# The last stage of a three-stage kernel: tanh left out of the gate, one subtraction on another engine, the last product turned around

## The chip, the cores and the metric

One Trainium2 chip, one of its cores. The core has TensorE (PE, whose weight loads are listed apart as PEld), VectorE (DVE), ScalarE (ACT), GpSimd (POOL) and SyncE (SP), which here only issues transfers. The metric is the device time of one execution in microseconds (us); less is better.

## What is computed

```python
# attention: q, k, v, f_logit are 4 x 8 x 768 x 48
f = sigmoid(f_logit)
state[t] = f[t][:, None] * state[t-1] + outer(k[t], v[t]);  y[t] = q[t] @ state[t]
x = y.transpose(0, 2, 1, 3).reshape(3072, 384)
# first feed-forward, 384 -> 1536 -> 384
x2 = ((x @ w_a) * (x @ w_b)) @ w_out
# second feed-forward, 384 -> 2048 -> 384
h = x2 @ w_in
out = (h - tanh(h)) @ w_out2
```

The inputs are q, k and v of size 0.1 (normal), f_logit 2 plus 0.5 times a normal, and weights scaled by the root of their length.

## The kernel before

All matrix products of the two feed-forward parts run in a form that splits each float32 operand into a high and a low part of the type float32r; a product is then three matmuls, high by high, high by low and low by high. `mm_split` (line 150) issues these three, so nearly every matmul of the trace carries line 150 and is told apart by its tiles. In the trace's names the operand that moves through the array stands first and the stationary one second: `o<-w_p,gh` moves the weights and holds the gate's high half.

The program runs attention and the first feed-forward together, block by block, and writes x2 in its two halves to DRAM (`xs`). The weights of the second feed-forward (`w_i`, `w_p`) are brought into the split form during the last of those blocks. Then comes the last stage, which the change is about. It is written in program order with no scheduler: each engine takes its instructions in the order of the loop.

The last stage has 96 steps: 6 blocks `o` of 512 tokens, times 16 slices `m` of 128 of the 2048 hidden columns. Step `i`, in order:

- PE makes `h`, 128 hidden columns by 512 tokens, in one PSUM bank: 9 matmuls (3 slices of the contraction, 3 of the split), in banks 0 to 3 by turns.
- `gelm_f32` (lines 84 to 96) makes h - tanh(h). ACT computes u = h squared (L86), tanh (L87) and two squares for the polynomial (L88, L89). POOL makes a mask of u over a threshold (L90). DVE makes xu (L91), h - tanh (L92), the two polynomial products v1 (L93) and v2 (L94), and puts h - tanh in place of the polynomial where the mask is set (L95).
- `gelm_lo` for step i - 1 makes the halves: ACT copies to `gh` (L560), POOL subtracts to `gl` (L561). There are 4 buffers of each.
- `o_group` for step i - 4 (`LAG`) adds the last product into 4 PSUM banks, one for each 128 of the 512 tokens: the gate's halves are stationary, the 384 columns of `w_p` move; 12 matmuls. At m = 15 ACT copies the 4 banks to `ob` (L582), and SP writes each to the output (L584).

One `ob` holds 64 tokens of each of two rows of the batch, so a write to the output has a shape of 2 by 64 by 384. The output has a row for each token.

A flag `okf` says whether the chunked form of attention was safe (the smallest product of decays). It is computed in the last block of the first feed-forward; each engine reads it (L711) and, where it is 0, a slow exact path runs instead.

Of the kernel before, what the change touches and what calls it, by code (L numbers as in the profile page):

```python
# [28 lines left out]
def tile_kernel(ctx: ExitStack, tc: tile.TileContext, q, k, v, f, w_a, w_b, w_out, w_in, w_out2, out):  # L29
    nc = tc.nc  # L30
    B, H, S, D = q.shape
    NT, DM = out.shape
# [51 lines left out]
    def gelm_f32(h, tmp):  # L84
# [10 lines left out]
        nc.vector.copy_predicated(v2, mk.bitcast(I32), t)  # L95
        return v2
# [55 lines left out]
    with tc.manual_schedule(), ExitStack() as p1:  # L152
# [237 lines left out]
        r2 = const.tile([1, 1], F32, name="r2")  # L390

        def flag():
            pr = att_bank("pr")
            nc.tensor.transpose(pr[0:1, 0:128], r1, ident)
            nc.vector.tensor_reduce(r2, pr[0:1, 0:128], mybir.AxisListType.X, ALU.min)
            nc.vector.tensor_scalar(okf, r2, P_MIN, None, ALU.is_ge)
# [134 lines left out]
        for jb in moe1(None):  # L531
# [16 lines left out]
            if jb == NBLK - 1 and slot == 2:  # L548
                flag()
# [6 lines left out]

        def gelm_lo(g):
# [13 lines left out]
        def o_group(i):  # L571
            o, m = divmod(i, MF2)
            if m == 0:
                po[o] = [bank(4 + g, f"o{g}")[:, :DM] for g in range(4)]
            g = G2.pop(i)
            for tg in range(4):
                cs = slice(128 * tg, 128 * tg + 128)
                mm_split(po[o][tg], [t[:, cs] for t in g], W["p", m], m == 0, m == MF2 - 1)
            if m == MF2 - 1:
                for tg in range(4):  # L580
                    ob = gp2.tile([128, DM], F32, tag="ob", name="ob", bufs=4)
                    nc.scalar.activation(ob, po[o][tg], ACTF.Copy)  # L582
                    c, hb = divmod(4 * o + tg, 2)
                    nc.sync.dma_start(  # L584
                        out=out.rearrange("(b s) d -> b s d", b=B)[2 * hb:2 * hb + 2, CH * c:CH * (c + 1), :],
                        in_=ob)

        for i in range(NO * MF2 + LAG):
            g = None
            if i < NO * MF2:  # L590
# [3 lines left out]
                ph = bank(i % 4, "h")  # L594
# [4 lines left out]
                g = gelm_f32(ph, lambda tag: gp2.tile([128, 512], F32, tag=tag, name=tag))  # L599
# [4 lines left out]
            gprev = g  # L604
            if i >= LAG:
                o_group(i - LAG)


    def general_path():
# [4 lines left out]
        yb = dpool.tile([B, S, H, D], F32, name="yb")  # L614
        flat = [x.rearrange("b h t d -> (b h) t d") for x in (q, k, v, f)]
        with ExitStack() as p3:
# [3 lines left out]
            with tc.For_i(0, S, TG) as t0:  # L620
# [22 lines left out]
                for eg in range(NE):  # L643
                    for b in range(B):
                        r0 = BH * eg + H * b
                        nc.sync.dma_start(
                            out=yb[b, ds(t0, TG), :, DE * eg:DE * (eg + 1)].rearrange("t h e -> h t e"),
                            in_=YG[r0:r0 + H])

        with ExitStack() as p4:  # L650
# [17 lines left out]
            with tc.For_i(0, NT // 128, 1) as it:  # L668
                x = sp.tile([128, H, D], F32, name="x")
                nc.sync.dma_start(  # L670
                    out=x,
                    in_=yb.rearrange("b t h d -> (b t) h d")[ds(it * 128, 128)],
                )
                xT = sp.tile([128, KT, 128], F32, name="xT")
                for kt in range(KT):
                    pt = pp.tile([128, 128], F32, tag="t", name="pt")
                    nc.tensor.transpose(
                        pt, x.rearrange("p h d -> p (h d)")[:, 128 * kt:128 * (kt + 1)], ident)
                    nc.vector.tensor_copy(xT[:, kt], pt)
                py = [pp.tile([128, 128], F32, name=f"py{d}") for d in range(KT)]  # L680
                for m in range(MF):
                    cs = slice(128 * m, 128 * (m + 1))
                    pa = pp.tile([128, 128], F32, tag="a", name="pa")
                    pb = pp.tile([128, 128], F32, tag="b", name="pb")
                    for p_, w_ in ((pa, FA), (pb, FB)):
                        for kt in range(KT):
                            nc.tensor.matmul(p_, w_[:, kt, cs], xT[:, kt], start=(kt == 0), stop=(kt == KT - 1))
                    asb = sp.tile([128, 128], F32, name="asb")
                    g = sp.tile([128, 128], F32, name="g")
                    nc.vector.tensor_copy(asb, pa)  # L690
                    nc.vector.tensor_tensor(g, asb, pb, ALU.mult)
                    for d in range(KT):
                        nc.tensor.matmul(py[d], FO[:, m, 128 * d:128 * (d + 1)], g,
                                         start=(m == 0), stop=(m == MF - 1))
                x2 = sp.tile([128, KT, 128], F32, name="x2")
                for d in range(KT):
                    nc.vector.tensor_copy(x2[:, d], py[d])
                po = pp.tile([128, DM], F32, tag="a", name="po")
                for m in range(MF2):
                    ph = pp.tile([128, 128], F32, tag="b", name="ph")  # L700
                    for kt in range(KT):
                        nc.tensor.matmul(ph, FI[:, kt, 128 * m:128 * (m + 1)], x2[:, kt],
# [40 lines left out]
```

## Time and profile before

| | |
|---|---|
| median of 3 runs | 1111.75 us (1111.71 to 1111.95) |
| the profiled execution: its own span | 1110.9 us |
| PE busy | 1018.1 us, 92% of the span |
| DVE busy | 826.0 us, 74% |
| ACT busy | 515.1 us, 46% |
| POOL busy | 506.8 us, 46% |
| mean granted TensorE clock | 0.962 of full speed |

The median of the runs is 0.85 us above the profiled span. Busy is the share in which an engine executes something; matmuls overlap in the pipeline, so a busy PE is not yet a PE at its peak. The stage at the end, from 653 us on, has its own limits, and the whole span's shares don't tell them.

### The profile page before, as it was taken

To read this page: it belongs to the slowest core of one execution; us is meant where nothing else is said; L and a number is where in the kernel's file an instruction comes from. 1 tells how busy PE (TensorE), PEld (TensorE's weight loads), DVE (VectorE), ACT (ScalarE), POOL (GpSimd) and SP (SyncE) were. 2 spreads that over 40 slices of the span, in tenths; PEclk is the share of its full clock that TensorE was granted. 3 is DMA by queue.
4 is the path that set the end of the run, shared out by engine and by line. 5 is a ranking of instruction groups with operands and counts; after the bars stand their busy time and mean duration, and the time that the engine had idled before them with its cause. 6 is when DMAs were issued, how large, how long until landed. Compare 5 with 4: busy or idle time off the path is not lost. (4 is left out here: it accounts for less than half of the span.)

```text
span 1110.9 us, 17772 instructions
## 1 busy us (share of the span) xinstructions
PE 1018.1 (92%) x6728; PEld 850.5 (77%) x6728; DVE 826.0 (74%) x1135; ACT 515.1 (46%) x979; POOL 506.8 (46%) x383
## 2 busy tenths in 40 slices
PE   7688889999999999999998879979989899899992
PEld 4567667888888888888776668869989799798891
DVE  8998887544444644444279989999999999999991
ACT  4433334333433333333333256666666666666661
POOL 3344543121212121212246557767767666677660
PEclk9789899999999999999999989989999999999997
DMA  6554455311412321140054440100100101000000
GB/s 129 145 142 120 129 144 138 62 30 23 114 30 43 92 45 30 36 102 1 15 190 141 149 146 1 58 10 21 57 29 1 59 28 58 22 8 1 29 1 31
DMA packets 134125, 72.41 MB, mean 65 GB/s; under 512 B 104912, under 2 KB 123344, under 8 KB 134032
## 3 DMA queue, kind: packets, MB, share of 16 engines
q1 hardware_dynamic: 132592, 69.23, 23.0%
q10 hardware_dynamic: 1440, 1.97, 1.0%
q8 instruction: 55, 0.90, 0.3%
q14 instruction: 38, 0.31, 0.1%
HBM read 55.05 MB, written 14.16 MB: 62 GB/s over the span
## 5 line engine op out<-in xcount | busy, mean ns | idle before, releaser
L491 POOL TENSOR_TENSOR gl<-gf,gh 128x512 fp32r<-128x512 f32 x72 | 93.1, 1293 | 365.2 <-ACT gh L490 365.2
L150 PE MATMUL o<-w_p,gh 128*128 128x384 f32 x768 | 203.2, 346 | 21.7 <-ACT ob L582 20.8
L150 PE MATMUL h<-x,w_i 128*128 128x512 f32 x864 | 214.4, 393 | 0.0
L90 POOL TENSOR_SCALAR mk<-u 128x512 f32<-128x512 f32 x96 | 179.3, 1868 | 22.9 <-ACT u L86 22.3
L150 PEld LDWEIGHTS h<-x,w_i 128*128 128x128 f32 x864 | 161.2, 188 | 29.4
L561 POOL TENSOR_TENSOR gl<-v,gh 128x512 fp32r<-128x512 f32 x96 | 124.6, 1298 | 112.4 <-ACT gh L560 112.2
L150 PE MATMUL b<-x,w_b 128*128 128x512 f32 x648 | 165.7, 400 | 10.2 <-DVE gf L489 9.7
L150 PE MATMUL a<-x,w_a 128*128 128x512 f32 x648 | 167.9, 403 | 5.8 <-DVE x L380 3.0
L150 PEld LDWEIGHTS o<-w_p,gh 128*128 128x128 f32 x768 | 145.2, 194 | 31.6 <-ACT ob L582 23.0
L150 PE MATMUL y<-gh,w_o 128*128 128x512 f32 x432 | 156.6, 417 | 4.5 <-ACT gh L490 4.5
L150 PEld LDWEIGHTS b<-x,w_b 128*128 128x128 f32 x648 | 121.4, 191 | 38.9 <-DVE gf L489 13.3
L150 PEld LDWEIGHTS a<-x,w_a 128*128 128x128 f32 x648 | 120.6, 191 | 33.2 <-DVE x L380 3.5
L93 DVE SCALAR_TENSOR_TENSOR v<-v,xu 128x512 f32<-128x512 f32 x96 | 144.4, 1505 | 0.0
L150 PE MATMUL o<-w_p,gl 128*128 128x384 f32 x384 | 133.6, 348 | 1.7 <-POOLq L712 0.7
L490 ACT ACTIVATE gh<-gf 128x512 fp32r<-128x512 f32 x72 | 45.5, 632 | 174.5 <-DVE gf L489 174.5
L560 ACT ACTIVATE gh<-v 128x512 fp32r<-128x512 f32 x96 | 60.7, 632 | 120.0 <-DVE v L95 119.4
L489 DVE TENSOR_TENSOR gf<-asb,b 128x512 f32<-128x512 f32 x72 | 49.3, 685 | 78.6 <-PE b L150 51.0
L150 PEld LDWEIGHTS y<-gh,w_o 128*128 128x128 f32 x432 | 85.1, 197 | 24.2 <-ACT gh L490 5.0
L94 DVE SCALAR_TENSOR_TENSOR v<-v,v 128x512 f32<-128x512 f32 x96 | 84.8, 883 | 10.0
L484 ACT ACTIVATE asb<-a 128x512 f32<-128x512 f32 x72 | 42.6, 592 | 104.7 <-PE a L150 82.1
L150 PE MATMUL y<-gl,w_o 128*128 128x512 f32 x216 | 88.3, 409 | 0.6 <-POOL gl L491 0.6
L95 DVE COPY_PREDICATED v<-mk,t 128x512 f32<-128x512 int32 x96 | 76.9, 801 | 9.9
(106 smaller groups left out, 1550.2 us busy)
## 6 DMA issues: line engine op xcount, KB each, us to landing
wst<-in_moe_w_out_dram SPq DMA_DIRECT2D x28, 384.0 KB
x<-xs SPq DMA_DIRECT2D x12, 768.0 KB
wst<-in_moe_w_in_dram SPq DMA_DIRECT2D x16, 384.0 KB
Tv<-in_v_dram SPq DMA_DIRECT2D x48, 96.0 KB
xs<-oh SPq DMA_DIRECT2D x18, 256.0 KB
xs<-ol SPq DMA_DIRECT2D x18, 256.0 KB
out_dram<-ob SPq DMA_DIRECT2D x24, 192.0 KB
Tf<-in_f_logit_dram SPq DMA_DIRECT2D x44, 96.0 KB
```

Source lines behind the costliest of these rows:

```text
L90: nc.gpsimd.tensor_scalar(mk, u, TANH_THR2, None, ALU.is_gt)
L93: nc.vector.scalar_tensor_tensor(v1, v1, Q_Y1, xu, ALU.add, ALU.mult)
L94: nc.vector.scalar_tensor_tensor(v2, v2, Q_Y2, v1, ALU.add, ALU.mult)
L95: nc.vector.copy_predicated(v2, mk.bitcast(I32), t)
L150: nc.tensor.matmul(dst, l_, r_, start=(first and i == 0), stop=(last and i == 2))
L484: nc.scalar.activation(asb, pb, ACTF.Copy)
L489: nc.vector.tensor_tensor(gf, asb, pab[1], ALU.mult)
L490: nc.scalar.activation(gh, gf, ACTF.Copy)
L491: nc.gpsimd.tensor_tensor(gl, gf, gh.bitcast(F32), ALU.subtract)
L560: nc.scalar.activation(gh, g, ACTF.Copy)
L561: nc.gpsimd.tensor_tensor(gl, g, gh.bitcast(F32), ALU.subtract)
```

## The change

Four things are done to the last stage:

- the gate uses the polynomial alone (`gelm_small`): tanh, mask, subtraction and selection are left out. The square of h also gives its sum over the 512 tokens (`accum_out`), one column of `usum` for each step. Where the greatest of these sums is over the threshold, the flag is cleared and the slow exact path runs. The flag moves to the end of the stage (`flag_rows` after step 96, `flag` one later);
- the subtraction to `gl` is made by DVE, no longer by POOL;
- the last product has the weights stationary and the gate's halves moving: 3 banks of 128 output columns by 512 tokens, 9 matmuls of 512 columns. `h` gets 5 banks;
- the output is stored transposed, 384 rows of 3072 tokens in the order of the blocks; each write is 128 rows by 512 tokens. The order of the tokens is put back outside the device's time.

The slow path is adapted to the new layout; it is not shown.

```diff
+    def gelm_small(h, tmp, total):
+        u, v1, v2, xu = (tmp(x) for x in ("u", "v1", "v2", "xu"))
+        nc.scalar.activation(u, h, ACTF.Square, accum_out=total)
+        nc.scalar.activation(v1, u, ACTF.Square, bias=bias1)
+        nc.scalar.activation(v2, u, ACTF.Square, bias=bias2)
+        nc.vector.scalar_tensor_tensor(xu, u, Q4, h, ALU.mult, ALU.mult)
+        nc.vector.scalar_tensor_tensor(v1, v1, Q_Y1, xu, ALU.add, ALU.mult)
+        nc.vector.scalar_tensor_tensor(v2, v2, Q_Y2, v1, ALU.add, ALU.mult)
         return v2
...
-        def flag():
-            pr = att_bank("pr")
-            nc.tensor.transpose(pr[0:1, 0:128], r1, ident)
+        def flag_rows(usum):
+            nc.vector.tensor_reduce(ru, usum, mybir.AxisListType.X, ALU.max)
+            nc.vector.scalar_tensor_tensor(ru, ru, TANH_THR2, r1, ALU.is_le, ALU.mult)
+
+        def flag(pr):
+            nc.tensor.transpose(pr[0:1, 0:128], ru, ident)
             nc.vector.tensor_reduce(r2, pr[0:1, 0:128], mybir.AxisListType.X, ALU.min)
-            nc.vector.tensor_scalar(okf, r2, P_MIN, None, ALU.is_ge)
+            nc.vector.tensor_scalar(okf, r2, 0.5, None, ALU.is_ge)
...
-            if jb == NBLK - 1 and slot == 2:
-                flag()
+                nc.vector.tensor_scalar(r1, r1, P_MIN, None, ALU.is_ge)
...
             nc.scalar.activation(gh, g, ACTF.Copy)
-            nc.gpsimd.tensor_tensor(gl, g, gh.bitcast(F32), ALU.subtract)
+            nc.vector.tensor_tensor(gl, g, gh.bitcast(F32), ALU.subtract)
             return gh, gl
 
         LAG = 4
+        NHB = 5
...
             if m == 0:
-                po[o] = [bank(4 + g, f"o{g}")[:, :DM] for g in range(4)]
+                po[o] = [bank(NHB + d, f"o{d}") for d in range(KT)]
             g = G2.pop(i)
-            for tg in range(4):
-                cs = slice(128 * tg, 128 * tg + 128)
-                mm_split(po[o][tg], [t[:, cs] for t in g], W["p", m], m == 0, m == MF2 - 1)
-            if m == MF2 - 1:
-                for tg in range(4):
-                    ob = gp2.tile([128, DM], F32, tag="ob", name="ob", bufs=4)
-                    nc.scalar.activation(ob, po[o][tg], ACTF.Copy)
-                    c, hb = divmod(4 * o + tg, 2)
-                    nc.sync.dma_start(
-                        out=out.rearrange("(b s) d -> b s d", b=B)[2 * hb:2 * hb + 2, CH * c:CH * (c + 1), :],
-                        in_=ob)
+            for d in range(KT):
+                cs = slice(128 * d, 128 * d + 128)
+                mm_split(po[o][d], [t[:, cs] for t in W["p", m]], g, m == 0, m == MF2 - 1)
+                if m == MF2 - 1:
+                    ob = gp2.tile([128, 512], F32, tag="ob", name="ob", bufs=3)
+                    nc.scalar.activation(ob, po[o][d], ACTF.Copy)
+                    nc.sync.dma_start(out=out[128 * d:128 * (d + 1), 512 * o:512 * (o + 1)], in_=ob)
...
-                ph = bank(i % 4, "h")
+                ph = bank(i % NHB, "h")
...
-                g = gelm_f32(ph, lambda tag: gp2.tile([128, 512], F32, tag=tag, name=tag))
+                g = gelm_small(ph, lambda tag: gp2.tile([128, 512], F32, tag=tag, name=tag), usum[:, i:i + 1])
...
+            if i == NO * MF2 + 1:
+                flag_rows(usum)
+            elif i == NO * MF2 + 2:
+                flag(bank(0, "pr"))
             if i >= LAG:
                 o_group(i - LAG)
...
-_OUTS = [((3072, 384), 'float32')]
+_OUTS = [((384, 3072), 'float32')]
```

The next rows are what the built programs hold, without any time. On VectorE, in the middle of the last stage, one step before:

```order
L91 SCALAR_TENSOR_TENSOR xu<-u,h 128x512
L92 TENSOR_TENSOR t<-h,t 128x512
L93 SCALAR_TENSOR_TENSOR v_7572<-v_7572,xu 128x512
L94 SCALAR_TENSOR_TENSOR v_7573<-v_7573,v_7572 128x512
L95 COPY_PREDICATED v_7573<-mk,t 128x512
```

and a step of the changed program, with the subtraction ahead of it:

```order
L576 TENSOR_TENSOR gl<-v_8296,gh 128x512
L103 SCALAR_TENSOR_TENSOR xu<-u,h 128x512
L104 SCALAR_TENSOR_TENSOR v_8361<-v_8361,xu 128x512
L105 SCALAR_TENSOR_TENSOR v_8362<-v_8362,v_8361 128x512
L576 TENSOR_TENSOR gl<-v_8329,gh 128x512
```

Five instructions have become four, and the fourth works on the gate of the step before.

On TensorE, the first step with a last product, before (the last `h` ahead of it, the product, and the next `h`):

```order
L150 MATMUL h<-x_5607,w_i_5814 128x512 x9
L150 MATMUL o_6476<-w_p_5665,gh 128x384 x2
L150 MATMUL o_6476<-w_p_5665,gl 128x384
L150 MATMUL o_6477<-w_p_5665,gh 128x384 x2
L150 MATMUL o_6477<-w_p_5665,gl 128x384
L150 MATMUL o_6478<-w_p_5665,gh 128x384 x2
L150 MATMUL o_6478<-w_p_5665,gl 128x384
L150 MATMUL o_6479<-w_p_5665,gh 128x384 x2
L150 MATMUL o_6479<-w_p_5665,gl 128x384
L150 MATMUL h<-x_5607,w_i_5857 128x512 x9
```

and now:

```order
L160 MATMUL h<-x_5605,w_i_5812 128x512 x9
L160 MATMUL o_6445<-gh,w_p_5663 128x512
L160 MATMUL o_6445<-gl,w_p_5663 128x512
L160 MATMUL o_6445<-gh,w_p_5663 128x512
L160 MATMUL o_6446<-gh,w_p_5663 128x512
L160 MATMUL o_6446<-gl,w_p_5663 128x512
L160 MATMUL o_6446<-gh,w_p_5663 128x512
L160 MATMUL o_6447<-gh,w_p_5663 128x512
L160 MATMUL o_6447<-gl,w_p_5663 128x512
L160 MATMUL o_6447<-gh,w_p_5663 128x512
L160 MATMUL h<-x_5605,w_i_5855 128x512 x9
```

Twelve matmuls of 384 columns have become nine of 512, and the gate is what moves.

On SyncE, the end of the program before (`x` loads of the last block, the last writes, the branch on the flag):

```order
L584 DMA out_dram<-ob 2x64x384 x4
L527 DMA x_9111<-xs_83 128x1536
L527 DMA x_9111<-xs_84 128x1536
L584 DMA out_dram<-ob 2x64x384 x12
L712 COMPARE_AND_BRANCH
```

and now:

```order
L541 DMA x_8515<-xs_83 128x1536
L541 DMA x_8515<-xs_84 128x1536
L598 DMA out_dram<-ob 128x512 x6
L736 TENSOR_LOAD okf
L736 ISA x2
L598 DMA out_dram<-ob 128x512 x3
L737 COMPARE_AND_BRANCH
```

The read of the flag now stands ahead of the last three writes; before, it stood much earlier.

## Rows read from the trace of the kernel before

**Rows 1.** The page: span, then busy us (share) xinstructions.

```profile
span 1110.9 us, 17772 instructions
PE 1018.1 (92%) x6728; PEld 850.5 (77%) x6728; DVE 826.0 (74%) x1135; ACT 515.1 (46%) x979; POOL 506.8 (46%) x383
```

**Rows 2.** Busy time, granted clock and DMA by window, within the last stage.

```profile
core 0: us, PE busy (x) PEld busy (x) DVE busy (x) ACT busy (x) POOL busy (x), PEclk, DMA share, GB/s
...
750.00:800.00 50.00, 50.00 (x252) 45.34 (x252) 47.72 (x57) 32.69 (x58) 35.84 (x23) 1.00 0.12 43
```

**Rows 3.** Who waited for whom, 660 to 1088 us: total, times, longest.

```profile
ACT gh L560 <- DVE v L95: 119.4, 85, 3.6
...
PE o L150 <- ACT ob L582: 20.8, 5, 8.2
```

**Rows 4.** Timeline of one step: start, duration, engine, instruction.

```profile
781.74 0.67 DVE L91 SCALAR_TENSOR_TENSOR xu<-u,h 128x512 f32<-128x512 f32 x1
...
782.33 0.68 DVE L92 TENSOR_TENSOR t<-h,t 128x512 f32<-128x512 f32 x1
...
782.59 1.29 POOL L561 TENSOR_TENSOR gl<-v,gh 128x512 fp32r<-128x512 f32 x1 [1.27 <-ACT gh L560]
...
782.93 1.51 DVE L93 SCALAR_TENSOR_TENSOR v<-v,xu 128x512 f32<-128x512 f32 x1
...
784.54 0.91 DVE L94 SCALAR_TENSOR_TENSOR v<-v,v 128x512 f32<-128x512 f32 x1
785.55 0.76 DVE L95 COPY_PREDICATED v<-mk,t 128x512 f32<-128x512 int32 x1
...
786.20 0.67 DVE L91 SCALAR_TENSOR_TENSOR xu<-u,h 128x512 f32<-128x512 f32 x1
```

**Rows 5.** Timeline, first and last step: v1 and v2 with POOL idle.

```profile
658.32 0.68 DVE L93 SCALAR_TENSOR_TENSOR v<-v,xu 128x512 f32<-128x512 f32 x1
...
1085.34 0.69 DVE L94 SCALAR_TENSOR_TENSOR v<-v,v 128x512 f32<-128x512 f32 x1
```

**Rows 6.** ScalarE's groups by line and shape, 630 to 1111 us: busy us, mean ns.

```profile
L88 ACT ACTIVATE v<-u,bias 128x512 f32<-128x512 f32 x96 | 69.6, 725 | 0.0
L89 ACT ACTIVATE v<-u,bias 128x512 f32<-128x512 f32 x96 | 69.4, 723 | 0.0
L560 ACT ACTIVATE gh<-v 128x512 fp32r<-128x512 f32 x96 | 60.7, 632 | 120.0 <-DVE v L95 119.4
...
L86 ACT ACTIVATE u<-h 128x512 f32<-128x512 f32 x96 | 56.5, 589 | 31.3 <-PE h L150 31.2
```

**Rows 7.** TensorE's timeline, a step of the last stage.

```profile
674.43 2.24 PE L150 MATMUL h<-x,w_i 128*128 128x512 f32 x9
676.51 0.52 PE L150 MATMUL o<-w_p,gh 128*128 128x384 f32 x2
...
678.61 2.24 PE L150 MATMUL h<-x,w_i 128*128 128x512 f32 x9
```

**Rows 8.** TensorE's timeline, first feed-forward: nine matmuls each of a, b, y.

```profile
560.49 2.22 PE L150 MATMUL a<-x,w_a 128*128 128x512 f32 x9
562.54 2.20 PE L150 MATMUL b<-x,w_b 128*128 128x512 f32 x9
564.58 0.39 PE L150 MATMUL y<-gh,w_o 128*128 128x512 f32 x1
...
566.62 0.62 PE L150 MATMUL a<-x,w_a 128*128 128x512 f32 x2
```

**Rows 9.** Timeline where the last stage starts: first x2 store, first h, first product.

```profile
651.78 0.33 SPq L465 DMA_DIRECT2D xs<-oh  x1
...
653.48 10.64 PE L150 MATMUL h<-x,w_i 128*128 128x512 f32 x45
...
663.96 0.51 PE L150 MATMUL o<-w_p,gh 128*128 128x384 f32 x2
```

**Rows 10.** The chain that ended last: start, us, what.

```profile
1089.00 2.02 PE o L150 x10
1091.02 0.02 issue
1091.04 0.49 ACT ob L582
```

**Rows 11.** Windows: x2's stores, and the end (last columns: clock, DMA share, GB/s).

```profile
652.00:653.00 1.00, 1.00 (x3) 0.77 (x3) 0.48 (x1) 0.56 (x1) 0.09 (x1) 0.50 0.38 145
...
655.00:656.00 1.00, 1.00 (x6) 0.81 (x5) 0.34 (x1) 0.00 (x1) 0.00 (x0) 1.00 1.02 375
...
1102.00:1104.00 2.00, 0.00 (x0) 0.00 (x0) 0.00 (x0) 0.00 (x0) 0.00 (x0) 0.50 0.13 51
...
1108.00:1109.00 1.00, 0.00 (x0) 0.00 (x0) 0.00 (x0) 0.00 (x0) 0.00 (x0) 0.50 0.05 17
```

More of the change, by code (lines that the diff above doesn't have):

```diff
@@ L31, in tile_kernel @@
     B, H, S, D = q.shape
-    NT, DM = out.shape
+    DM, NT = out.shape
     DFF = w_a.shape[1]
@@ L95, in gelm_f32 @@
         nc.vector.copy_predicated(v2, mk.bitcast(I32), t)
+        return v2
+    def gelm_small(h, tmp, total):
[6 more added lines that the diff above has]
+        nc.vector.scalar_tensor_tensor(v2, v2, Q_Y2, v1, ALU.add, ALU.mult)
         return v2
@@ L390, in tile_kernel @@
         r2 = const.tile([1, 1], F32, name="r2")
-        def flag():
-            pr = att_bank("pr")
-            nc.tensor.transpose(pr[0:1, 0:128], r1, ident)
+        ru = const.tile([128, 1], F32, name="ru")
+        def flag_rows(usum):
[3 more added lines that the diff above has]
+            nc.tensor.transpose(pr[0:1, 0:128], ru, ident)
             nc.vector.tensor_reduce(r2, pr[0:1, 0:128], mybir.AxisListType.X, ALU.min)
-            nc.vector.tensor_scalar(okf, r2, P_MIN, None, ALU.is_ge)
+            nc.vector.tensor_scalar(okf, r2, 0.5, None, ALU.is_ge)
         gens = {i: attn_step(i) for i in range(PRO + 1)}
@@ L555, in tile_kernel @@
         gp2 = p1.enter_context(tc.tile_pool(name="gp2", bufs=2))
+        usum = gp2.tile([128, (NT // 512) * MF2], F32, name="usum", bufs=1)
         def gelm_lo(g):
@@ L613, in general_path @@
         BH = B * H
-        yb = dpool.tile([B, S, H, D], F32, name="yb")
+        yb = dpool.tile([S // TG, B, TG, H, D], F32, name="yb")
         flat = [x.rearrange("b h t d -> (b h) t d") for x in (q, k, v, f)]
@@ L619, in general_path @@
             nc.vector.memset(S4, 0.0)
-            with tc.For_i(0, S, TG) as t0:
+            with tc.For_i(0, S // TG, 1) as ti:
+                t0 = ti * TG
                 LQ, LK, LF, LG = (fp.tile([128, TG, D], F32, name=nm) for nm in ("LQ", "LK", "LF", "LG"))
@@ L646, in general_path @@
                         nc.sync.dma_start(
-                            out=yb[b, ds(t0, TG), :, DE * eg:DE * (eg + 1)].rearrange("t h e -> h t e"),
+                            out=yb[ds(ti, 1), b, :, :, DE * eg:DE * (eg + 1)].rearrange("o t h e -> h (o t) e"),
                             in_=YG[r0:r0 + H])
@@ L667, in general_path @@
                         w_bits(dst[:, kk, c0:c0 + n0].bitcast(I32), st[:, :2 * n0])
[L668 to L685, printed above, removed]
-                        for kt in range(KT):
[L687 to L691, printed above, removed]
-                    for d in range(KT):
[L693 to L702, printed above, removed]
-                                         start=(kt == 0), stop=(kt == KT - 1))
-                    g = gelm_f32(ph, lambda tag: sp.tile([128, 128], F32, tag=tag, name=tag))
-                    nc.tensor.matmul(po, g, FP[:, m, :], start=(m == 0), stop=(m == MF2 - 1))
-                ob = sp.tile([128, DM], F32, name="ob")
-                nc.vector.tensor_copy(ob, po)
-                nc.sync.dma_start(out=out[ds(it * 128, 128), :], in_=ob)
@@ L740 @@
     r = _run(nc, [arrays], core_ids=[0])
-    got = tuple(r.results[0][f"out_{i}_dram"] for i in range(len(_OUTS)))
-    return got[0]
+    got = r.results[0]["out_0_dram"].reshape(384, 12, 4, 64)
+    return _np.ascontiguousarray(got.transpose(2, 1, 3, 0)).reshape(3072, 384)
```

47 lines of the change are left out of this document (added).

## The prediction

> **What bounds the kernel now.** I read the page first: PE is busy for 92% of the span [rows 1], which would make TensorE the bound. That is a mean over stages, so I went to the last stage alone. There DVE is busy 47.72 of 50 us while ACT has 32.69 and POOL 35.84 [rows 2]. PE counts as busy throughout, but its pipeline stretches the records of matmuls that wait; what decides is who waits for whom. ACT's copy to gh waits 119.4 us in all for DVE's last instruction of the gate [rows 3]. So the engine that never waits is DVE.
>
> The timeline of one step gives its pace: from one xu to the next, 781.74 to 786.20, are 4.46 us [rows 4]. 96 steps at 4.46 are 428 us. Of PE's own work a step holds nine matmuls of 512 columns, 674.43 to 676.51 or 2.08 us, and twelve of 384, to 678.61 or 2.10 us [rows 7]: 4.18 us. PE is thus only 0.28 us a step behind DVE, and that is the first thing to see: taking work from DVE can give no more than this before PE is the bound.
>
> The stage starts at 653.48 with 45 matmuls of h, the first product starts at 663.96 [rows 9], the last matmul ends at 1091.02 and the last copy at 1091.53 [rows 10]. Then 19.4 us pass to the end of the span in which no engine computes. The windows show why: the writes of the output move 51 GB/s with a DMA share of 0.13, about two of 16 engines, until after 1108 us, whereas the stores of x2, 128 rows by 512 columns, ran at 375 GB/s and a share of 1.02 [rows 11].
>
> **DVE's part.** Out go h - tanh, 0.60 us from start to start, and the selection, 0.65 us [rows 4]. In comes gl. What v1 costs is the point that needs care: it takes 1.51 us in a step, but it began while POOL's subtraction still ran, to 783.88, and ended 0.56 us after that [rows 4]; with POOL idle it took 0.68 us in the first step, and v2 took 0.69 us in the last [rows 5]. In the changed stage POOL has no work, so I take 0.69 us for each of the four: 4 x 0.69 = 2.8 us a step, against PE's 4.15. The bound from the other side is the stretched row: if v1 and gl, both with two operands in SBUF, cost 1.61 us from start to start and v2 1.01 whatever POOL does, a step has 0.59 + 1.61 + 1.01 + 1.61 = 4.82 us. The row with POOL idle is the nearer one.
>
> **ACT's part.** Tanh goes. Left are 0.59 + 0.73 + 0.72 + 0.63 = 2.67 us [rows 6], and 18 copies of a bank at some 0.6 us over the stage, 0.1 us a step. What the sum over the tokens adds to the square is in no row: between nothing and a further pass over the tile, 0.59 us. Even that leaves 3.4 us, under PE's step, so both ends cost nothing; from 1.4 us it would be the bound.
>
> **PE's part.** A step now has 18 matmuls of 512 columns. Nine take 2.08 us for h [rows 7]. For the new product, weights stationary and the gate moving, the nearest row is y of the first feed-forward, which has just this form: 564.58 to 566.62, 2.04 us; a and b there take 2.05 and 2.04 [rows 8]. Bounds are 2.04 and 2.10 us for nine; I take 2.075, nearer to the last stage's own row, as its engines are busier than the first's. Columns are the same in total as before (12 x 384 = 9 x 512), so the turned product itself gives nearly nothing; it pays through the stores. From the first product on there are 91 groups for h and 96 for o: 187 x 2.075 = 388.0 us (381.5 to 392.7). From 663.96 that ends at 1052.0, and 0.2 us for the flag's transpose and the last drain make 1052.2.
>
> The Trainium skill, page "TensorE: Matmul & The Clock Gate", section "Wait — 56ns, not 53.3ns?", gives 215.7 ns for a matmul of 512 columns at full clock, which as an estimate is 1.94 us for nine. The rows show 2.04 to 2.08 us, at a granted clock of 1.00 in the last stage [rows 2], which is the level of 2.4 GHz; they decide. By the page the stage would end 25 us earlier; that is a rival below.
>
> **What is hidden.** gl on DVE stands behind gh on ACT, which stands behind the next step's squares: square, two more squares, gh and gl are 0.59 + 0.73 + 0.72 + 0.63 + 0.69 = 3.4 us after the next h. The product that needs it comes three steps later, over 12 us, so neither is waited for. If ACT stalls, gh is late first, then gl, then the product. The flag's rows come after the last gl; their transpose stands ahead of the second-last product on PE. From the last h to that place PE has three products, 6.2 us; DVE needs some 4.5 us for the last gate and its gl and 0.5 for two small instructions. It is in time by about 1 us; if not, PE loses what is missing, below 1 us. Behind the flag's read on SP stand the last three writes; the flag is known a product earlier, 2 us ahead of the first of them, so the read is over. Without that cover the writes come later by about as much. The early flag's removal frees PE, DVE and SP of some 0.1 to 0.5 us; I count nothing.
>
> **The end.** The three copies of a block are now issued as each bank is done, so after the last matmul one copy of some 0.6 us is left. From the issue of x2's first store to data moving took about 0.85 us (651.78 to 652.6: the share in 652 to 653 is 0.38 [rows 9, 11]); 256 KB at 375 GB/s are 0.7 us. From the last data (about 1108.5 [rows 11]) to the end of the span were 2.4 us. 0.6 + 0.85 + 0.7 + 2.4 = 4.6 us against 19.9 now.
>
> **The sum.** 1052.2 + 4.6 = 1056.8, that is 54 us under the span of 1110.9: 39 from the step (96 x 0.3, the start and the stalls at the end of the stage) and 15 from the stores. The median of the runs lies 0.85 us over the span, which makes 1057.7, so 1058.
>
> **Rivals.**
> - Copies at the end of a block. The three banks of o are single, so the first product of a block waits for the copies of the last. Before, five such waits cost PE 20.8 us [rows 3], while DVE set the pace and they cost nothing; now each would count. Against it: the first copy is through about 3.3 us after h is ready (squares 2.0, gh 0.6, copy 0.6), and PE comes back to that bank after a product and the next h, 4.15 us. It decides when ACT is later than by 0.9 us. All of it: 1058 + 20.8 = 1079. The Trainium skill, "Perfetto Trace Analysis", section "Matmuls", says that independent groups of matmuls should rotate through banks so that emptying one overlaps the next group; these don't. By that rule the trace shows the waits, but not that they must stay. Chance 0.10.
> - The writes stay slow: rows of 512 tokens lie 12 KB apart in the output, and if they again use two engines, three writes of 256 KB at 51 GB/s take 15 us in place of about 1.5: 1072. Against it: x2's stores have such a stride too. Chance 0.06.
> - PE runs faster: if the extra 13 to 15 ns in each matmul come from traffic that the change takes away, nine take 1.94 us, and 187 x 0.135 = 25 us go: 1033. Against it: in the first feed-forward DVE was often idle, and nine still took 2.04. Chance 0.05.
> - DVE stays the bound and gets slower: the 4.82 us above. 96 x (4.82 - 4.46) = +35, less 15 for the stores: 1131. It decides where a step on DVE passes 4.46 + 15 / 96 = 4.62 us. Against it stand [rows 5]. Chance 0.03.
> - The flag falls and the slow path runs: it decides at a sum of squares over 0.4225 in any of the 96 columns. From the reference's inputs I work out at most 3.2e-5. The path has 768 steps of five DVE instructions at 0.68 us or more, over 2600 us more. Chance 0.01.
>
> **How the numbers follow.** The forecast has 0.75, with a range of its own of 1051 to 1064 (PE's bounds, 1 us for the flag, 2 for the end). Ends up to the slow writes and part of the copies' waits give 1048 to 1077, which leaves out PE's faster pace, most of the copies' case and the slow ones, together under 0.2. A measurement here tells 0.2%, 2.2 us, from no change. All cases but DVE and the flag are faster: 0.95; 0.01 for a pace that ends just where it was; 0.04 slower.
>
> **What would show it.** DVE under 70% busy in the stage, v1 near 0.69 us, POOL without work; groups of nine matmuls every 2.04 to 2.10 us without a gap from 664 us on; no wait of PE for ob; the writes of the output at a DMA share near 1; some 5 us from the last matmul to the end. A pace above 4.3 us a step, waits on L597 at block ends, or a tail of 15 us would make me wrong, each in its own term.

## The result and the profile after

The changed kernel takes 1060.79 us (median of four runs, 1058.78 to 1061.16); the kernel before took 1111.73 beside it. The ratio is 0.9535, with a 95% interval of 0.9519 to 0.9551. The forecast was 1058, with a range of 1048 to 1077. The profiled execution has a span of 1059.2 us in a run of 1060.94, so 1.7 us lie outside the span.

I read the last stage first, as before. The windows of the changed kernel (busy us of PE, PEld, DVE, ACT, POOL, then granted clock, DMA share and GB/s) show 50 us in the middle of the stage, and the end:

```profile
750.00:800.00 50.00, 50.00 (x220) 40.78 (x218) 32.40 (x49) 32.33 (x64) 0.00 (x0) 1.00 0.13 48
1052.00:1053.00 1.00, 1.00 (x5) 0.47 (x3) 0.00 (x0) 0.84 (x2) 0.00 (x0) 1.00 0.00 0
1053.00:1054.00 1.00, 0.00 (x0) 0.00 (x0) 0.00 (x0) 0.60 (x1) 0.00 (x0) 1.00 0.90 342
1054.00:1055.00 1.00, 0.00 (x0) 0.00 (x0) 0.00 (x0) 0.00 (x0) 0.00 (x0) 1.00 1.01 371
1055.00:1056.00 1.00, 0.00 (x0) 0.00 (x0) 0.00 (x0) 0.00 (x0) 0.00 (x0) 1.00 0.29 100
1056.00:1057.00 1.00, 0.00 (x0) 0.00 (x0) 0.00 (x0) 0.00 (x0) 0.00 (x0) 1.00 0.05 14
```

DVE fell from 47.72 [rows 2] to 32.40 of 50 us, and POOL has no instruction. In the tail the writes now move up to 371 GB/s at a share near 1, where it was 51 at 0.13 [rows 11]. Who waits for whom has turned round. The waits of 640 to 1060 us (total, times, longest):

```profile
ACT u L100 <- PE h L160: 133.3, 86, 1.6
DVE xu L103 <- ACT u L100: 113.2, 91, 1.4
ACT ob L597 <- PE o L160: 5.4, 1, 5.4
```

Before, ACT waited 119.4 us for DVE and PE 20.8 for ob [rows 3]. Now ACT waits for PE, DVE waits for ACT, and PE has no wait for ob at all. TensorE sets the pace. The groups of DVE and ACT in the stage (busy us, mean ns; then idle time before them):

```profile
L105 DVE SCALAR_TENSOR_TENSOR v<-v,v 128x512 f32<-128x512 f32 x96 | 66.5, 693 | 10.3 <-ACT gh L575 0.5
L104 DVE SCALAR_TENSOR_TENSOR v<-v,xu 128x512 f32<-128x512 f32 x96 | 66.5, 692 | 10.0
L103 DVE SCALAR_TENSOR_TENSOR xu<-u,h 128x512 f32<-128x512 f32 x96 | 66.0, 687 | 113.2 <-ACT u L100 113.2
L576 DVE TENSOR_TENSOR gl<-v,gh 128x512 fp32r<-128x512 f32 x96 | 65.9, 686 | 0.2 <-ACT gh L575 0.2
...
L101 ACT ACTIVATE v<-u,bias 128x512 f32<-128x512 f32 x96 | 69.6, 725 | 3.1
L102 ACT ACTIVATE v<-u,bias 128x512 f32<-128x512 f32 x96 | 68.1, 709 | 0.6 <-DVE gl L576 0.6
L575 ACT ACTIVATE gh<-v 128x512 fp32r<-128x512 f32 x96 | 59.2, 616 | 0.5 <-DVE v L105 0.5
L100 ACT ACTIVATE u<-h 128x512 f32<-128x512 f32 x96 | 57.5, 599 | 134.0 <-PE h L160 133.3
L100 ACT ACTIVATION_READ_ACCUMULATOR u<-h 128x1 f32 x96 | 18.6, 194 | 0.0
```

A step has 2.76 us on DVE (four instructions) and 2.84 on ACT. The last of the ACT rows answers the open price of the sum over the tokens: its read-out is an instruction of its own, 194 ns, and the square itself takes 599 ns where it took 589 [rows 6]. The timeline shows a step of PE (start, duration), and the flag at the end:

```profile
770.99 2.25 PE L160 MATMUL h<-x,w_i 128*128 128x512 f32 x9
773.07 0.39 PE L160 MATMUL o<-gh,w_p 128*128 128x512 f32 x1
...
775.16 2.22 PE L160 MATMUL h<-x,w_i 128*128 128x512 f32 x9
...
1047.13 0.16 DVE L405 SCALAR_TENSOR_TENSOR ru<-ru,r 128x1 f32<-128x1 f32 x1
...
1048.54 0.27 PE L408 MATMUL pr<-ident,ru 128*1 128x128 f32 x1
```

From h to h are 4.17 us here. The first product starts at 665.42 and the last matmul at 1052.60, which for 187 groups of nine is 2.070 us each. The flag's row is ready at 1047.29, 1.25 us before PE comes to the transpose. The chain that ended last (start, us, what) runs through PE without a gap to the last copy:

```profile
1042.45 6.26 PE o L160 x27
...
1048.82 4.20 PE o L160 x18
...
1053.03 0.60 ACT ob L597
```

From there to the end of the span are 5.6 us, where it was 19.4. The three writes of the last block, issued at 1052.26, 1052.96 and 1053.66, took ever longer to land (us; the first is the shortest, the last the longest):

```profile
DMA to landing us min/median/max: 2.0/2.8/3.6
```

### The profile page after: what moved, and what is told of

Its sections match the earlier page's. It is cut to its first block, busy times and chain, and to the rows that moved or that the text cites. A ratio compares the mean times of both kernels' runs of the same rounds, so it can differ in the third digit from the quotient of the medians.

```text
span 1059.2 us, 16687 instructions
## 1 busy us (share of the span) xinstructions
PE 997.1 (94%) x6438; PEld 801.2 (76%) x6440; DVE 674.5 (64%) x1042; ACT 485.2 (46%) x973; POOL 205.2 (19%) x191
## 4 chain that ended last, share of the span: by engine, by line
PE 79%; DVE 11%; issue 5%; DMA 2%; ACT 1%; POOL 1%; ACTq 0%; SPq 0%; DVEq 0%; POOLq 0%
PE o L160 19%; PE h L160 19%; PE y L160 11%; PE a L160 11%; PE b L160 10%; DVE wc L81 3%; DVE wc L80 3%; PE pt L281 2%; PE yy L376 2%; PE sc L332 1%; PE uu L359 1%; PE pk L336 1%; DVE wc L82 1%; DVE gf L503 1%; DVE PRE L308 1%
## 5 line engine op out<-in xcount | busy, mean ns | idle before, releaser
L160 PE MATMUL o<-gh,w_p 128*128 128x512 f32 x576 | 194.7, 393 | 0.0
L103 DVE SCALAR_TENSOR_TENSOR xu<-u,h 128x512 f32<-128x512 f32 x96 | 66.0, 687 | 113.2 <-ACT u L100 113.2
L160 PEld LDWEIGHTS o<-gh,w_p 128*128 128x128 f32 x576 | 108.2, 188 | 24.7 <-issue 0.2
L100 ACT ACTIVATE u<-h 128x512 f32<-128x512 f32 x96 | 57.5, 599 | 134.0 <-PE h L160 133.3
L160 PE MATMUL o<-gl,w_p 128*128 128x512 f32 x288 | 113.1, 393 | 0.0
L82 DVE SCALAR_TENSOR_TENSOR wc<-wst,wc 128x384 int32<-128x384 int32 x68 | 74.6, 1096 | 2.4
L105 DVE SCALAR_TENSOR_TENSOR v<-v,v 128x512 f32<-128x512 f32 x96 | 66.5, 693 | 10.3 <-ACT gh L575 0.5
L104 DVE SCALAR_TENSOR_TENSOR v<-v,xu 128x512 f32<-128x512 f32 x96 | 66.5, 692 | 10.0
L101 ACT ACTIVATE v<-u,bias 128x512 f32<-128x512 f32 x96 | 69.6, 725 | 3.1
```

The lines of the kernel that those rows point to most:

```text
L82: nc.vector.scalar_tensor_tensor(dst, lo, 29, dst, ALU.logical_shift_right, ALU.bitwise_or)
L100: nc.scalar.activation(u, h, ACTF.Square, accum_out=total)
L101: nc.scalar.activation(v1, u, ACTF.Square, bias=bias1)
L103: nc.vector.scalar_tensor_tensor(xu, u, Q4, h, ALU.mult, ALU.mult)
L104: nc.vector.scalar_tensor_tensor(v1, v1, Q_Y1, xu, ALU.add, ALU.mult)
L105: nc.vector.scalar_tensor_tensor(v2, v2, Q_Y2, v1, ALU.add, ALU.mult)
```

## The experiments

Times are medians, and the ratio is to the kernel before, on the same chip.

**One part alone.** Three runs take the change apart. `stores_only` leaves the kernel before as it is, but writes each bank in two halves of 64 rows.

```diff
-                    nc.sync.dma_start(
-                        out=out.rearrange("(b s) d -> b s d", b=B)[2 * hb:2 * hb + 2, CH * c:CH * (c + 1), :],
-                        in_=ob)
+                    for r in range(2):
+                        nc.sync.dma_start(
+                            out=out.rearrange("(b s) d -> b s d", b=B)[2 * hb + r, CH * c:CH * (c + 1), :],
+                            in_=ob[64 * r:64 * r + 64])
```

> The kernel before with one edit: each write of 2 by 64 by 384 is issued as two writes of 64 by 384, one for each row of the batch. Theory (a write whose outermost dimension is 2 keeps to two of the 16 DMA engines; that makes the tail): the DMA share at the end rises from 0.13 to well over 0.5, the time from the last matmul to the end falls from 19.9 to some 7 us, and the time to about 1098 (1095 to 1101). Rival (rows of 1536 bytes, or the place in the output, make the writes slow): the share stays near 0.13 and the time at 1111.

1103.55 us, 0.9926 [0.9904, 0.9948]. The transposed layout isn't needed for this part of the gain: a shape whose outermost size is 64 in place of 2 is enough to leave the slow writes. Its windows in the tail, and then the issues on SP:

```profile
1090.00:1092.00 2.00, 0.00 (x0) 0.00 (x0) 0.00 (x0) 0.24 (x1) 0.00 (x0) 1.00 0.51 120
1092.00:1094.00 2.00, 0.00 (x0) 0.00 (x0) 0.00 (x0) 0.00 (x0) 0.00 (x0) 0.75 0.68 160
```

```profile
1088.70 6.59 SPq L585 DMA_DIRECT2D out_dram<-ob  x8
```

The share is 0.51 to 0.68 instead of 0.13 [rows 11]. The time from the last matmul to the end is 12.0 us; 19.9 it was, and 7 were expected. SP issues the eight writes over 6.59 us, and the data end 1.3 us after the last issue; as far as the rows tell, the issuing is the limit now. The splitting didn't make it longer: the four writes of before were issued over 8.13 us. So the gain was nearly 9 us and not 14: right in kind, too large in size. The Trainium skill, "DMA: Bandwidth & Descriptors", section "Rules for kernel authors", says that an outermost dimension of c below 16 confines a transfer to at most c engines. The trace agrees: an outermost 2 gave a share of 0.13, about two of 16, and 128 gives 1.01.

`gate_only` is the kernel before with `gelm_small` and the late flag; the subtraction stays on POOL, product and stores stay as they were.

```diff
...
-                g = gelm_f32(ph, lambda tag: gp2.tile([128, 512], F32, tag=tag, name=tag))
+                g = gelm_small(ph, lambda tag: gp2.tile([128, 512], F32, tag=tag, name=tag), usum[:, i:i + 1])
...
+            if i == NO * MF2 + 1:
+                flag_rows(usum)
+            elif i == NO * MF2 + 2:
+                flag(bank(0, "pr"))
```

> The kernel before with only the gate by polynomial and the late flag; the subtraction stays on POOL, product and stores as before. Theory (DVE's five instructions set the pace, then PE does, and the tail is the stores'): a step falls from 4.46 to PE's 4.18 us, the last matmul ends near 1055, the tail stays at 19.9 us, the time is about 1076 (1072 to 1080). Rival one (the turned product earns PE time as well): a step stays above 4.25 us and the time above 1082. Rival two (POOL's subtraction goes on stretching v1 and so holds DVE): v1 stays at 1.5 us, which is 3.3 us a step for DVE in all, so that it would show in v1's mean and not in the time.

1076.70 us, 0.9678 [0.9661, 0.9694], as expected. This is the greater part of the change. The gate lost instructions on DVE, ACT and POOL at once, and they were not tried one by one; that DVE's are the ones that count is read from the trace of before, in which DVE goes from one step to the next without a wait [rows 4] and waits 1.8 us in all 96 gates together. The timeline of `gate_only`, DVE and POOL:

```profile
762.59 0.69 DVE L105 SCALAR_TENSOR_TENSOR v<-v,v 128x512 f32<-128x512 f32 x1
...
762.94 1.51 POOL L577 TENSOR_TENSOR gl<-v,gh 128x512 fp32r<-128x512 f32 x1 [2.68 <-ACT gh L576]
```

`product_only` is the changed kernel with the gate of before, its subtraction on POOL, and a flag that holds the decays alone.

```diff
...
-            nc.vector.tensor_tensor(gl, g, gh.bitcast(F32), ALU.subtract)
+            nc.gpsimd.tensor_tensor(gl, g, gh.bitcast(F32), ALU.subtract)
...
-                g = gelm_small(ph, lambda tag: gp2.tile([128, 512], F32, tag=tag, name=tag), usum[:, i:i + 1])
+                g = gelm_f32(ph, lambda tag: gp2.tile([128, 512], F32, tag=tag, name=tag))
```

> The changed kernel with the old gate (tanh, mask, selection) and the subtraction on POOL: only the turned product with its stores, 5 banks for h and the late place of the flag are left; the sum over the tokens is left out, and the flag tells of the decays alone. Theory: DVE's pace of 4.46 us a step as before, a tail of some 6 us: about 1098 (1095 to 1101). Rival (turning the product frees PE time that counts): under 1090.

1102.36 us, 0.9905 [0.9885, 0.9924], just above. DVE is back at 47.37 of 50 us and the step at 4.48. The 4 us missing are at the end, in PE's timeline and in the window of 1088 to 1092:

```profile
1088.28 0.37 PE L407 MATMUL pr<-ident,ru 128*1 128x128 f32 x1 [3.32 <-DVE ru L404]
1088.30 0.77 PE L160 MATMUL o<-gh,w_p 128*128 128x512 f32 x1
```

```profile
1088.00:1092.00 4.00, 3.73 (x10) 2.94 (x11) 0.64 (x4) 0.63 (x1) 1.27 (x1) 0.50 0.03 8
```

With DVE late, the flag's transpose waits 3.32 us, and both last products stand behind it on PE. The granted clock is then 0.50, the level of 1.2 GHz, so that the matmuls come every 0.43 us. SP's issue of the very last write took 1.80 us besides, where 0.33 is usual; why isn't known. The 1.25 us of margin of the changed kernel are what keeps the wait from it.

**The subtraction.** `gl_pool` is the changed kernel with this one instruction back on POOL (the first two changed lines of the diff above).

> The changed kernel with one edit: the subtraction to gl goes back to POOL. Theory (with the gate by polynomial DVE has over 1 us of slack a step, and gl is needed three steps later): no change, 1059 to 1063, though v1 grows from 0.69 us towards 1.5 where it meets POOL's subtraction. Rival (the moved subtraction is part of the gain, since POOL stretches DVE and gl comes late): PE waits for gl, and the time is above 1065.

1059.37 us, 0.9527 [0.9510, 0.9545]: the same as the changed kernel. But it didn't go as expected inside. Its groups in the stage:

```profile
L576 POOL TENSOR_TENSOR gl<-v,gh 128x512 fp32r<-128x512 f32 x96 | 143.0, 1490 | 251.4 <-ACT gh L575 251.4
...
L105 DVE SCALAR_TENSOR_TENSOR v<-v,v 128x512 f32<-128x512 f32 x96 | 66.4, 692 | 10.1 <-ACT v L102 0.2
```

v1 doesn't meet POOL's subtraction here at all; v2 does, ahead of it by 0.35 us as in `gate_only` (764.55 against 764.90), and v2 keeps its 692 ns. It is POOL's subtraction that grows, from 1.29 [rows 4] to 1.49 us. Before, gl began at 782.59 and v1 at 782.93, and v1 waited [rows 4]; in `gate_only` v2 began at 762.59 and gl at 762.94, and gl waited. The trace of before has both orders behind the end of a block:

```profile
751.17 0.69 DVE L93 SCALAR_TENSOR_TENSOR v<-v,xu 128x512 f32<-128x512 f32 x1
...
751.53 1.48 POOL L561 TENSOR_TENSOR gl<-v,gh 128x512 fp32r<-128x512 f32 x1
...
751.96 1.60 DVE L94 SCALAR_TENSOR_TENSOR v<-v,v 128x512 f32<-128x512 f32 x1
```

The subtraction, second to v1, takes 1.48 us, and v2, second to the subtraction, 1.60. Of these pairs the instruction that comes second pays. The Trainium skill says this of these two engines ("SBUF — State Buffer", section "Who interferes with whom"): a DVE instruction with two inputs in SBUF contends with a GpSimd instruction that reads SBUF, and the order of issue decides who blocks. The traces agree for v1, v2 and the subtraction. Before, v2 also ran beside POOL's mask, from 783.85 to 785.78: it took 0.91 us and ended ahead of it [rows 4], so that pair shows no waiting for the other's end.

**How much room ACT has.** In the changed kernel ACT has 2.84 of 4.14 us. `act_2` adds two passes of 0.53 us to each step, between the squares and gh; `act_4` adds four. The output doesn't use them.

```diff
         nc.scalar.activation(v2, u, ACTF.Square, bias=bias2)
+        for k in range(2):
+            nc.scalar.activation(tmp(f"t{k}"), h, ACTF.Tanh)
         nc.vector.scalar_tensor_tensor(xu, u, Q4, h, ALU.mult, ALU.mult)
```

> The changed kernel with two more passes of ACT in each step (tanh of h into tiles that nothing reads), between the squares and the copy to gh. Theory (ACT is busy 2.68 of 4.14 us a step, and the copies at the end of a block have under a microsecond to spare): the pace stays PE's, ACT rises to some 3.7 us a step, and PE waits for a bank at the block ends by at most a few tenths of a us each, under 2 us in all: 1059 to 1063. Rival (the single banks of the product make block ends costly as soon as ACT is late): five waits of 1 us and more, above 1066.

> The same with four more passes. Theory: ACT then has 2.7 + 4 x (0.48 to 0.59) = 4.6 to 5.0 us of work a step and is the bound: 96 x (0.5 to 0.9) more, 1108 to 1146. Rival (more of ACT's time overlaps than its busy time tells): below 1090.

1110.84 us, 0.9987 [0.9978, 0.9997], and 1201.52 us, 1.0793 [1.0775, 1.0811]. My theory, that ACT costs nothing until its busy time passes PE's, missed by 50 and by more than 55 us. The waits of `act_2` say why:

```profile
DVE xu L105 <- ACT t L104: 163.6, 88, 3.7
ACT v L102 <- DVE gl L578: 67.8, 77, 1.0
...
PE o L162 <- ACT ob L599: 27.5, 5, 7.6
```

And its timeline, ACT and DVE, from one second square to the next:

```profile
751.50 0.71 ACT L102 ACTIVATE v<-u,bias 128x512 f32<-128x512 f32 x1
752.12 1.06 ACT L104 ACTIVATE t<-h 128x512 f32<-128x512 f32 x2
...
753.21 0.69 DVE L105 SCALAR_TENSOR_TENSOR xu<-u,h 128x512 f32<-128x512 f32 x1 [3.45 <-ACT t L104]
753.93 0.69 DVE L106 SCALAR_TENSOR_TENSOR v<-v,xu 128x512 f32<-128x512 f32 x1
754.66 0.69 DVE L107 SCALAR_TENSOR_TENSOR v<-v,v 128x512 f32<-128x512 f32 x1
755.27 0.68 DVE L578 TENSOR_TENSOR gl<-v,gh 128x512 fp32r<-128x512 f32 x1
...
755.99 0.72 ACT L102 ACTIVATE v<-u,bias 128x512 f32<-128x512 f32 x1 [0.22 <-DVE gl L578]
```

xu now waits for the passes; gl stands on DVE behind v2; and the next second square writes the buffer of v2's tile that this gl reads, since there are two. Square, passes, xu, v1, v2, gl and back make a loop of 4.49 us (751.50 to 755.99), with neither ACT (40.18 of 50 us) nor DVE (28.42) full. xu uses nothing of the passes, but it stands behind them in the program and reads h as they do; it starts 0.03 us after the last of them. The span is longer than the changed kernel's by 49.1 us, and 48.8 of these lie between the first and the last second square (433.8 us instead of 385.0). The first six steps cost 9.0: the changed kernel runs them at 2.0 to 3.5 us, as PE is ahead there, and the loop can't. The ten steps at the ends of blocks cost 11.4, as the product waits for ob there and PE falls behind in its turn; these are the five waits of my first rival, brought on at will. The other 79 cost 0.36 each, 28.4 in all. `act_4` has the same loop at 5.48 us: its second squares start at 750.09 and 755.57.

`act_2_late` puts two passes behind gh, where they read the gate g in place of h, and gives v2's tile three buffers.

```diff
             nc.scalar.activation(gh, g, ACTF.Copy)
+            for k in range(2):
+                nc.scalar.activation(gp2.tile([128, 512], F32, tag="t", name="t"), g, ACTF.Tanh)
...
-                g = gelm_small(ph, lambda tag: gp2.tile([128, 512], F32, tag=tag, name=tag), usum[:, i:i + 1])
+                g = gelm_small(ph, lambda tag: gp2.tile([128, 512], F32, tag=tag, name=tag, bufs=3 if tag == "v2" else 2), usum[:, i:i + 1])
```

> After the change, with the same two extra passes of the scalar engine per step as in act_2, but placed behind the copy gh (so xu does not wait for them) and with three buffers instead of two for v2's tile. The output is the same. ACT's work per step is the same as in act_2: about 2.68 + 2 x 0.53 = 3.74 us of the 4.14 that PE needs. Theory (act_2's 4.48 us a step came from a loop through ACT, DVE and v2's two buffers, and not from ACT's busy time): the loop is open, PE sets 4.14 to 4.16 us a step again, the waits of xu for t and of v2 for gl are gone, and the time is that of the changed kernel, 1059 to 1065. Rival (ACT's added work costs wherever it stands, by its share or by its neighbours' access to memory): over 1090.

1061.73 us, 0.9534 [0.9518, 0.9551]: the time of the changed kernel. In its windows ACT is busier than in `act_2`:

```profile
750.00:800.00 50.00, 49.99 (x218) 40.50 (x217) 31.73 (x48) 43.93 (x87) 0.00 (x0) 1.00 0.12 47
```

So ACT's busy time costs nothing up to 88% here, and the loop was the cause. Whether the place, the other operand or the third buffer alone would do wasn't tried.

**TensorE by itself.** `pe_alone` makes the gate for the first step alone and multiplies all 96 steps by it; PE's work is the same.

```diff
...
-                g = gelm_small(ph, lambda tag: gp2.tile([128, 512], F32, tag=tag, name=tag), usum[:, i:i + 1])
+                g = gelm_small(ph, lambda tag: gp2.tile([128, 512], F32, tag=tag, name=tag), usum[:, 0:1]) if i == 0 else g0
...
-            if gprev is not None:
-                G2[i - 1] = gelm_lo(gprev)
-            gprev = g
+            if i == 0:
+                g0 = g
+                half0 = gelm_lo(g)
+            G2[i] = half0
```

> The changed kernel with the gate computed for the first step alone: all 96 products take its two halves. ACT, DVE and POOL have nothing to do for the other 95 gates; the output is that of the wrong gates. Theory (a matmul of 512 columns that has a weight load of its own takes 227 to 233 ns here whatever the other engines do): nine matmuls stay at 2.04 to 2.08 us, the time at 1056 to 1062. Rival (the other engines' traffic in SBUF and PSUM stretches the matmuls from 216 ns): nine fall towards 1.94 us and the time towards 1036.

1055.12 us, 0.9486 [0.9470, 0.9502]. In its timeline a matmul follows the last by 226 to 227 ns in the mean of nine:

```profile
772.33 2.20 PE L160 MATMUL h<-x,w_i 128*128 128x512 f32 x9
774.37 0.39 PE L160 MATMUL o<-gh,w_p 128*128 128x512 f32 x1
```

Nine take 2.04 us, with DVE at nothing and ACT at 1.79 of 50 us. The work of the other engines thus costs 0.03 us in nine, 187 x 0.03 = 5.6 us in the stage, and no more. The rival of 1.94 us for nine, which the Trainium skill's 215.7 ns ("TensorE: Matmul & The Clock Gate", section "Wait — 56ns, not 53.3ns?") would give, isn't reached even so.

**What is left.** With PE full from 665 us on, what remains lies ahead of the stage. In the last block of the first feed-forward, 32 weights of the last stage are converted, one a slot. A window of the changed kernel there, and then three of `spread_22`, which converts 22 there and the other ten in the first steps of the last stage:

```profile
610.00:620.00 10.00, 8.28 (x36) 6.46 (x35) 9.79 (x12) 3.60 (x7) 6.54 (x7) 1.00 0.44 128
```

```diff
-                w_tick(3 * MF + slot - 3)
+                w_tick(3 * MF + (2 * (slot - 3)) // 3)
```

> The changed kernel with fewer of the last stage's weights converted in the block before: 22 in place of 32, the other 10 one a step in the last stage, where DVE now has slack. Theory (DVE's conversions set the pace of the last block of the first feed-forward, about 2 us each): 10 x 2 = 20 us less there, 3 to 8 us more in the ten steps that take a conversion over PE's pace: 1043 to 1050. Rival one (something else, the loads of the weights for instance, sets the pace of that block): 1058 to 1062. Rival two (the last stage waits for late weights): above 1062.

```profile
610.00:620.00 10.00, 10.00 (x46) 8.25 (x45) 9.66 (x13) 3.41 (x7) 5.27 (x5) 1.00 0.39 120
...
640.00:650.00 10.00, 4.57 (x11) 3.33 (x11) 9.34 (x15) 7.05 (x15) 2.02 (x2) 0.71 0.40 142
...
670.00:680.00 10.00, 8.86 (x36) 6.60 (x36) 9.45 (x15) 5.92 (x12) 2.04 (x2) 1.00 0.26 80
```

1050.35 us, 0.9445 [0.9430, 0.9461]. There DVE (9.8 of 10 us) was the bound and PE waited; with fewer conversions PE is full and the first h comes at 629.73 instead of 654.99. Of these 25 us some 15 are lost again: the first products wait for gh and gl, the clock is 0.71 in 640 to 650, and each step with a conversion takes about 4.88 us, with the same wait of the second square for gl (20.1 us in 15 waits). Three more runs went after this loss. `spread_26` converts 26 ahead and six behind:

```diff
-                w_tick(3 * MF + slot - 3)
+                w_tick(3 * MF + (4 * (slot - 3)) // 5)
```

> After the change, with 26 of the 32 conversions of the last stage's weights in the last block of the first feed-forward (32 in the changed kernel, 22 in spread_22) and 6 in the first steps of the last stage. spread_22 began its last stage 25 us earlier for ten conversions moved, 2.5 each, and gave back some 15, 1.5 each. Theory (the gain and the loss both go by the number moved): first h 15 us earlier than in the changed kernel, a loss of 6 to 9, 1051 to 1055. Rival (the loss is mostly that of the first steps, the wait for the first gate and the half clock behind it, whatever the number): 1054 to 1059. Rival (the loss comes only where the tenth step meets the product's lag): 1045 to 1050.

1049.97 us, 0.9433 [0.9413, 0.9452]: below the theory's 1051, at the end of the second rival. The first h is at 638.63, later by 8.9 us than in `spread_22`, and all of this comes back. `spread_22_paced` goes back to 22, spaces the other ten, three in four steps and behind the gate's low half, and has the third buffer:

```diff
...
-            if i >= 1:
-                w_tick(nconv[0] + 1)
             if gprev is not None:
                 G2[i - 1] = gelm_lo(gprev)
+            if i >= 1:
+                w_tick(3 * MF + 23 + (3 * (i - 1)) // 4)
```

> As spread_22, but the ten conversions left for the last stage come three in four steps instead of one in each, behind the gate's low half instead of in front of it, and v2's tile has three buffers. DVE's work per step is then 2.77 + 0.75 x 1.46 = 3.87 us, with v2 lengthened beside POOL by 0.35 about 4.15, against 4.85 in the conversion steps of spread_22 and 4.14 on PE. First h as in spread_22 (630). Theory (spread_22 lost its 15 us to DVE's 4.85 us steps with gl at their end): the loss is halved, 1040 to 1046. Rival (it was lost to the transition itself: the wait for the first gates and the half clock): 1048 to 1052, as spread_22.

1050.22 us, 0.9443 [0.9424, 0.9461], no better than `spread_22`. Between 650 and 678 us the steps do run without loss. But PE's timeline has this:

```profile
641.47 0.65 PE L160 MATMUL o<-gh,w_p 128*128 128x512 f32 x1 [2.21 <-ACT gh L575]
643.57 0.80 PE L160 MATMUL o<-gl,w_p 128*128 128x512 f32 x1 [1.45 <-DVE gl L576]
...
694.24 4.44 PE L160 MATMUL h<-x,w_i 128*128 128x512 f32 x9 [4.30 <-ACT w_i L145]
```

The transition still costs two waits, and a weight converted too late costs 4.30 us more, nine matmuls then taking 4.44 us instead of 2.25. The theory was right for the steps and wrong for the sum. `spread_26_paced` has the six of `spread_26` in this pace:

```diff
...
+            if i >= 1:
+                w_tick(3 * MF + 27 + (3 * (i - 1)) // 4)
```

> As spread_26, with the edits of spread_22_paced: the six conversions left come three in four steps, behind the gate's low half, and v2's tile has three buffers. In spread_26 six steps of the last stage each lost 0.61 us or so between the first and the second matmul of a product (0.83 to 0.88 where 0.23 is usual), 3.7 us in all, and the first one 1.6; the half clock at the stage's start lies before it. In spread_22_paced those steps ran at PE's pace and the loss was the wait of the first product and a weight that was converted too late by 4.3 us, which a smaller number left over avoids. Theory: 3 to 4 us less than spread_26, 1045 to 1048. Rival (what is saved in the steps is lost in the first product's wait or by the clock, as in spread_22_paced): 1049 to 1051.

1047.54 us (five runs, 1046.87 to 1048.78), 0.9425 [0.9412, 0.9439], inside what was expected. It is faster than both kernels, 65 us below the one before and 13 below the changed one.

## Why the prediction was right, step by step

The mechanism was right: DVE sets the pace before, PE after, and the slow writes go. From the first product to the end of the last matmul the time fell from 427.1 us to 387.6, and from there to the end of the span from 19.9 to 6.2. The sum came out 3.2 us short: the start, the tail and the time outside the span were each too small, and a pace taken a little too dear gave some of it back, which is luck.

- **DVE's pace**, 2.8 us for four instructions of 0.69: measured 2.76. The row with POOL idle [rows 5] was the right one. The reason given was half of it: in `gl_pool` POOL works, and v2 beside its subtraction still takes 0.69, as DVE's instruction comes first there.
- **ACT**, 2.67 us and nothing to 0.59 for the sum: measured 2.84, of which 0.19 for the sum's read-out. That even the dearer end costs nothing was argued from busy time. `act_2` shows this argument to be unsafe: with a busy time still under PE's, a loop over two engines and two buffers set 4.49 us. It held here because ACT's wait for gl comes to 0.6 us in all.
- **PE's groups**, 2.075 us for nine: measured 2.070. `pe_alone` puts the floor at 2.04, which was the lower bound.
- **What is hidden**: the flag had 1.25 us of margin, predicted about 1. `product_only` shows what lies beyond it, 3.3 us of wait and a lower clock. No product waited for gh or gl once the stage ran.
- **The start** was carried over as 663.96 and came at 665.42. The changed kernel is behind before the last stage; the first `a` of the first feed-forward starts at 47.97 instead of 46.73 us. `gl_pool`, with the same order up to the last stage, has its first product at 662.64, so this term moves by as much from one execution to another.
- **The end of PE** thus came at 1053.0 instead of 1052.2: 1.5 later by the start, 0.9 earlier by the pace.
- **The tail** is the term that was mis-sized: 4.6 us were expected from the last matmul's end, and it took 6.2. Its copy took 0.60 as said. But I let one write of 256 KB land, and all three of the last block were in flight: the first was issued at 1052.26, nothing moved before 1053, and the windows after that show 342 + 371 + 100 + 14 = 827 KB, the three writes and some 40 KB beside them. The first of the three took 2.0 us from issue to landing, the last 3.6; these 1.6 us are what was missing.
- **Outside the span** lie 1.7 us instead of 0.85. This is no effect of the change. In every execution on record for which both figures are known, of the kernel before, of the changed one and of all the others, time and span lie 1.66 to 1.84 us apart. The 0.85 set the median of three executions against a span that, by this gap, belongs to another and slower one. The 0.8 of PE's end, the 1.6 of the tail and 0.9 here make the 3.2 us between 1057.7 and 1060.94.

The rivals: copies at a block's end didn't happen (no wait of PE for ob), and `act_2` shows that they do happen once the gate's pace falls behind PE's. Slow writes are excluded by the share of 1.01, the faster PE by `pe_alone`, a DVE that stays the bound by 32.40 of 50 us, and the slow exact path by the time itself.

The shares of the gain: the gate alone gave 35.6 us, product and stores alone 10.0, all of it together 51. The missing 5 are, as far as the rows tell, the 3.32 us that the late flag cost `product_only`, the lower clock behind it, and its one long issue of 1.80 us.

## What to carry to other kernels

Work taken from the bound pays only down to the next engine; here that was 0.3 of 1.7 us a step, and the rest of DVE's relief paid nothing. Before calling an engine free by its busy share, follow one step's dependences through its buffers: a loop through two engines and two buffers can set the pace while both have room, and here a later place and an additional buffer together opened it. A last transfer's time begins with what is still in flight before it, so count the block's writes together. Set a time against a span only where both come from the same execution.

## What the runs showed of the hardware that was not expected

- The sum that a ScalarE instruction accumulates is read out by an instruction of its own, 194 ns each, 18.6 us over the stage.
- Of a two-input DVE instruction and a POOL subtraction that overlap, the second pays: 1.48 to 1.68 us for DVE's instead of 0.69, or 1.48 to 1.51 for POOL's instead of 1.29.
- 512-column matmuls with a new stationary operand each follow every 226 to 227 ns with the other engines silent, and nine take 0.03 us more with DVE and ACT at 65%.
- SP's issue of a write most often took 0.34 us for 128 by 512, 0.59 for 64 by 384 and 0.61 for 2 by 64 by 384 (medians in the changed kernel, `stores_only` and before); single issues took up to 0.37, 1.68 and 5.61 there, and 1.80 in `product_only`. What lengthens these isn't shown.
- The granted clock stood at 0.50 in 1088 to 1092 of `product_only`, behind the transpose's wait of 3.32 us, and in 694 to 699 of `spread_22_paced`, behind a wait of 4.30 us, where nine matmuls took 4.44 us.
